# A fused Fourier filter and two expert layers: the start of the kernel loaded and ordered in another way

## The chip, the cores and the metric

The kernel runs on one core of a Trainium2 chip. The metric is device time in microseconds (us) for one launch; the smaller the better. The engines are TensorE (PE: matmuls; PEld: its weight loads, which overlap them), VectorE (DVE), ScalarE (ACT), GpSimd (POOL) and SyncE (SP), which in this kernel does nothing but issue DMAs. Each engine works through its own queue in order. PSUM is the memory that matmuls write to, here eight banks of 128 x 512 f32; SBUF is the on-chip memory of 128 partitions.

## The reference

Three steps in a row, cut here to what matters: a Fourier transform along the sequence, a product with a complex filter, the transform back; then two expert layers, the first with a piecewise quadratic in the middle, the second with `silu`.

```python
X = np.fft.rfft(x, axis=1)                     # x: 2 x 3008 x 256
Y = X * (filt_r + 1j * filt_i)[None, :, :]
x = np.fft.irfft(Y, n=3008, axis=1).reshape(6016, 256)
h = x @ w_in                                   # 256 -> 2048
g = np.where(h >= 1, h, np.where(h <= -1, 0.0, (h + 1) ** 2 / 4))
x = g @ w_out                                  # 2048 -> 256
h = x @ w_in2
out = (h * (1 / (1 + np.exp(-h)))) @ w_out2
```

## The kernel before

The transform of length 3008 = 47 x 64 is done with small transform matrices. The work is cut into 32 **items** (`items`: 16 groups of 16 channels for each of two sequences). The first `HEAD` = 17 items form the **head** of the program and are the subject here; the other 15 are woven into the first expert layer later on. An item i of the head goes through these steps, each put at a time slot `t` of the table `agenda`:

- `load_x(i)` and `load_f(i)`: DMAs on SP. `x` is 96 partitions x 512 f32, the filter 64 partitions x 768 f32, 196.6 KB each. The filter is needed in both halves of the partitions. In the head only its first half is loaded, and `twin_f` (ACT) copies it to partitions 64 to 127. The 16 items of the first sequence load `x` straight into the large tile `Z1`; the filter has a ring of six buffers.
- `fwd_n1` (PE, matrix `fwd1`), `turn_fwd` (DVE, a transpose `t<-h`), `fwd_n2` (PE, matrix `fwd2`, a part of the constant tile `dft_sb`).
- `signs` (POOL) multiplies the filter's second part by the constant `sgn`, and `filter_` (DVE) multiplies by both filter parts, `y<-h,f`.
- `swap_add`: two copies on ACT (`s<-y`) swap the partition halves of the second product, and POOL adds them to the first (`y<-y,s`). For the last four items of the head (`LAST` = 4) it is left out, and `inv_n2` instead does two matmuls, one with the matrix `inv2_swap`, whose rows are swapped, and one with `inv2`.
- `inv_n2` (PE, `o_b<-y`), `turn_inv` (DVE, a transpose `Z<-o_b`).

When the head is done, four calls of `prep_x` (PE, `h<-dft_sb,Z`, with `inv1`) make the input of the first expert layer for two blocks of 502 tokens. Then the layer's **slots** follow, from `t = NB` = 24 on: in each, `up` makes 128 of the 2048 inner rows of a block (six matmuls, `h<-x,wh`), ACT and DVE form the quadratic, `split_g` splits the result into a rounded part `gh` and a rest `gl`, and `down` (six matmuls, `o_a<-gh`) adds to the output. `down` runs `LAG` = 5 slots behind `up`. The weights are converted from 64-bit words by `read_weight` (ACT, two operations), `form_weight` (DVE, three operations on `we` and `wa`, then POOL) and split by `split_weight` (ACT `wh`, then POOL `wl`).

The order on each engine is that of the code up to slot `HOLD`; from there the class `Planner` keeps the code's order on PE, and chooses the order on the other engines by its own estimate of when each operation can start and is due. `head_banks` in the diff adds two PSUM banks to the four that the ring `h` has. A DMA waits, beside its buffer, for a semaphore that an earlier DMA used: there are eight of them, so at most eight DMAs are under way.

Of the kernel before, what the change touches and what calls it, by code (L numbers as in the profile page):

```python
# [9 lines left out]
F32 = mybir.dt.float32  # L10
# [5 lines left out]
AF = mybir.ActivationFunctionType  # L16
# [10 lines left out]
K1 = N1 // 2 + 1  # L27
# [5 lines left out]
UTOK = 2 * N1  # L33
# [20 lines left out]
def _constants():  # L54
# [31 lines left out]
    dft[:, 256:384] = inv2.reshape(128, 128)  # L86
    dft[:, 384:384 + UTOK] = inv1.reshape(128, UTOK)
    dft[:, 384 + UTOK:384 + UTOK + K1] = sgn
    dft[:, 384 + UTOK + K1:] = np.roll(inv2.reshape(128, 128), 64, 0)
    return dft.astype(np.float32)  # L90


# [194 lines left out]
def tile_fft_conv_moe_moe(  # L287
# [11 lines left out]
    nc = Planner(tc.nc)  # L299
    ctx.enter_context(tc.manual_schedule())  # L300
    HEAD, LAG, EARLY = 17, 5, 12
    LAST = 4
# [19 lines left out]

    for tag in ("gh", "gl"):
        rings[tag] = [mp.tile([128, PMAX], F32R, tag=tag, name=f"{tag}_{i}", bufs=LAG - 1) for i in range(LAG - 1)]
    rings["ob"] = [mp.tile([128, PMAX], F32, tag="ob", name=f"ob_{i}", bufs=3) for i in range(3)]

    def make_ring(tag, n, pool, shape, dtype):
# [31 lines left out]

    nc.scalar.dma_start(fwd1, dft[:96, :128])  # L360
    fwd2 = dft_sb[:, 0:128]
    inv2 = dft_sb[:, 128:256]
    inv1 = dft_sb[:, 256:256 + UTOK]
    sgn = dft_sb[:, 256 + UTOK:]


    weights, cv = {}, {}
# [67 lines left out]
    def load_f(i):  # L435
        c, b = items[i]
        ft[i] = rot("f")
        for h in range(1 if i < HEAD else 2):
            nc.sync.dma_start(ft[i][h * 64:(h + 1) * 64], filt[c])

    def twin_f(i):

        if i < HEAD:
            nc.scalar.activation(ft[i][64:128], ft[i][0:64], AF.Copy)

    mats = {}

# [63 lines left out]
        st[i] = y.rearrange("p (d k) -> p d k", k=K1), v  # L513

    def swap_add(i):
        if HEAD - LAST <= i < HEAD:
            return
        y, v = st[i]
        yf = y.rearrange("p d k -> p (d k)")
        s = rot("s")  # L520
        nc.scalar.activation(s[0:64], v[64:128], AF.Copy)
        nc.scalar.activation(s[64:128], v[0:64], AF.Copy)
        nc.gpsimd.tensor_tensor(yf, yf, s, ALU.add)
        st[i] = y

    def inv_n2(i):
        z = zps[i % len(zps)][:, :, :K1]
        if HEAD - LAST <= i < HEAD:
# [587 lines left out]
    def at(t, fn, *args):  # L1116
        agenda.setdefault(t, []).append((fn, args))
# [5 lines left out]
    def plan_weight(t, m, f, pool):  # L1123
        at(t, fetch_weight, m, f)
        at(t + CR, read_weight, m, f)
        at(t + CF, form_weight, m, f)
        at(t + CS, lambda: split_weight(m, f, pool()))


    DONE = HEAD + 4  # L1130
    for i in range(HEAD):
        if i >= 3:
            at(i - 3, load_x, i)
        if i >= 2:
            at(i - 2, load_f, i)
    for t in range(DONE + 1):
        for fn, d in ((twin_f, 0), (fwd_n2, 2), (inv_n2, 4), (fwd_n1, 0), (turn_fwd, 1), (signs, 1), (turn_inv, 5), (filter_, 2), (swap_add, 2)):
            if 0 <= t - d < HEAD:
                at(t, fn, t - d)
    at(8, lambda: nc.sync.dma_start(inv2_swap, dft[:, 384 + UTOK + K1:]))  # L1140
    at(NB - P0, prep_x, 0, 0)
    at(NB - P1, prep_x, 1, 0)
    at(NB - P2, prep_x, 0, 1)
# [87 lines left out]
    open_dp("dpa", 2, 6, 3, 2)  # L1231
    warm = dp.tile([128, 512], BF16, name="warm", bufs=1)
    nc.vector.memset(warm, 0.0)
    ps = rot("h")
    for _ in range(WARM):
        nc.tensor.matmul(ps, warm[:, :128], warm, start=True, stop=True)
    clear_pads("a")
    load_x(0)
    load_x(1)
    nc.scalar.dma_start(dft_sb, dft[:, 128:384 + UTOK + K1])  # L1240

    nc.scalar.activation(warm[:, :1], warm[:, :1], AF.Silu)
    load_f(0)
    load_x(2)
    load_f(1)
    inv2_swap = dp.tile([128, 128], F32, name="inv2_swap", bufs=1)
# [7 lines left out]
    def stages(t):  # L1254
        nonlocal late
        if t == max(NB, DONE + 1):
            dctx.close()
# [10 lines left out]
        if t == END:  # L1268
# [121 lines left out]
```

## Time and profile before

| what | value |
|---|---|
| median of 3 runs | 1087.36 us (1086.96 to 1087.63) |
| the profiled execution: its own time | 1088.39 us |
| the profiled execution: span from first to last instruction | 1086.6 us |
| busy, as a share of the span | PE 99%, PEld 81%, DVE 85%, ACT 84%, POOL 21% |
| head and `prep_x` (first product to the first `up`) | 3.75 to 53.50 us |

The span is 1.8 us shorter than the execution's own time. The page's times start at the span's start. A row of the timeline gives the start, the length, the engine, the operation with output and inputs, and, in brackets, how long the engine sat idle before it and what ended that. An f32 matmul of the head shows as two records (x2). The ends of PE's records are modelled and overlap the next one, so the time a matmul takes is read from the distance of two starts.

### The profile page before, as it was taken

The numbers are of one execution on the slowest core, as the hardware profiler recorded it, in microseconds if no ns is written. First come the engines' busy times: TensorE is split into PE (matmuls) and PEld (weight loads), VectorE is DVE, ScalarE is ACT, GpSimd is POOL, SyncE is SP. The second block draws the span as 40 slices with busy tenths as digits, with TensorE's granted clock in tenths as the row PEclk, the third lists the DMA queues.
The fourth block names the chain that finished last, engine by engine and source line by source line (L and its number), as shares of the span: only waits on it lengthen the run. The fifth ranks groups of instructions, "written<-read, shape, count | busy, mean of one in ns | idle before, by whom it ended". The sixth has DMA issues, their size and how long they took to land.

```text
span 1086.6 us, 14688 instructions
## 1 busy us (share of the span) xinstructions
PE 1077.3 (99%) x4797; PEld 880.5 (81%) x4797; DVE 920.3 (85%) x1528; ACT 909.6 (84%) x1700; POOL 224.9 (21%) x208
## 2 busy tenths in 40 slices
PE   9999999999999999999999999999999999999997
PEld 4678888888888888887878878888888888888885
DVE  7989667877779786768887688999999999999988
ACT  6699778878778878879999889889889898889885
POOL 5656234666522110004433000000000000000000
PEclk9999999999999999999999999999999999999999
DMA  9634032435221000115686753433434333332401
GB/s 203 153 97 146 21 124 75 147 116 147 89 87 59 20 1 1 39 39 175 222 275 218 296 168 104 148 110 109 145 113 140 131 106 118 134 103 102 140 1 38
DMA packets 57884, 126.50 MB, mean 116 GB/s; under 512 B 6192, under 2 KB 30224, under 8 KB 57808
## 3 DMA queue, kind: packets, MB, share of 16 engines
q1 hardware_dynamic: 57552, 125.33, 35.9%
q8 instruction: 37, 0.61, 0.2%
q14 instruction: 39, 0.32, 0.1%
q10 hardware_dynamic: 256, 0.24, 0.1%
HBM read 94.35 MB, written 31.20 MB: 116 GB/s over the span
## 4 chain that ended last, share of the span: by engine, by line
PE 88%; DVE 5%; ACT 3%; DMA 1%; issue 1%; SPq 0%; POOL 0%; DVEq 0%; ACTq 0%
PE h L172 44%; PE o_a L172 24%; PE o_b L172 20%; DVE gl L172 1%; ACT gh L172 1%; DVE xr L172 1%; DVE y L172 1%; DMA f<-in_filt_dram 1%; ACT c L172 0%; ACT rawb L172 0%; DVE t L172 0%; SPq L172 0%; DMA inv_swap<-in_dft_dram 0%; DMA raw<-in_moe_w_in_dram 0%; DVE h L172 0%
## 5 line engine op out<-in xcount | busy, mean ns | idle before, releaser
L172 PE MATMUL h<-xr,ur 128*128 128x502 f32 (+1 forms) x816 | 227.6, 389 | 0.2
L172 PEld LDWEIGHTS h<-xr,ur 128*128 128x128 f32 x816 | 153.4, 189 | 33.3 <-ACT sl_g L172 0.8
L172 PE MATMUL o_a<-gh,wh 128*128 128x502 f32 (+1 forms) x395 | 154.4, 391 | 0.9 <-DVE sl_wh L172 0.7
L172 PE MATMUL o_a<-gl,wh 128*128 128x502 f32 (+1 forms) x395 | 154.2, 390 | 0.5 <-DVE gl L172 0.5
L172 PE MATMUL o_a<-gh,wl 128*128 128x502 f32 (+1 forms) x395 | 154.1, 390 | 0.0
L172 PE MATMUL o_b<-gh,wh 128*128 128x502 f32 (+1 forms) x292 | 114.2, 391 | 0.0
L172 PE MATMUL o_b<-gh,wl 128*128 128x502 f32 (+1 forms) x292 | 113.8, 390 | 0.0
L172 PE MATMUL o_b<-gl,wh 128*128 128x502 f32 (+1 forms) x292 | 113.7, 389 | 0.0
L172 ACT ACTIVATE gh<-sl_g 128x502 fp32r<-128x502 f32 (+1 forms) x141 | 87.4, 620 | 18.0 <-PE o_a L172 8.1
L172 DVE TENSOR_TENSOR gl<-sl_g,gh 128x502 fp32r<-128x502 f32 (+1 forms) x141 | 94.8, 673 | 8.9 <-ACT gh L172 8.7
L172 DVE TENSOR_TENSOR gl<-h,gh 128x502 fp32r<-128x502 f32 (+1 forms) x122 | 82.1, 673 | 12.7 <-ACT gh L172 11.6
L172 ACT ACTIVATE u<-h 128x502 f32<-128x502 f32 (+1 forms) x122 | 71.3, 585 | 23.4 <-PE h L172 22.6
L172 DVE SCALAR_TENSOR_TENSOR h<-u,h 128x502 f32<-128x502 f32 (+1 forms) x84 | 57.1, 681 | 39.5 <-ACT u L172 38.7
L172 PEld LDWEIGHTS o_a<-gh,wh 128*128 128x128 f32 x395 | 74.4, 188 | 17.1 <-ACT gh L172 1.5
L172 PEld LDWEIGHTS o_a<-gl,wh 128*128 128x128 f32 x395 | 74.4, 188 | 16.6 <-DVE gl L172 1.5
L172 PEld LDWEIGHTS o_a<-gh,wl 128*128 128x128 f32 x395 | 74.3, 188 | 15.2
L172 ACT ACTIVATE gh<-h 128x502 fp32r<-128x502 f32 (+1 forms) x122 | 71.3, 585 | 4.9 <-DVE h L172 1.6
L172 ACT ACTIVATE u<-u 128x502 f32<-128x502 f32 (+1 forms) x115 | 71.6, 623 | 2.9 <-DVE u L172 0.6
L172 POOL TENSOR_TENSOR w2s<-w2s 128x448 fp32r<-128x448 f32 x32 | 41.3, 1306 | 139.8 <-DVE w2s L172 114.7
L172 PE MATMUL h<-xb,wh 128*128 128x502 f32 (+1 forms) x212 | 65.7, 391 | 0.8 <-ACT g L172 0.8
L172 PEld LDWEIGHTS o_b<-gh,wh 128*128 128x128 f32 x292 | 55.0, 188 | 11.4 <-ACT o_b L172 0.4
L172 PEld LDWEIGHTS o_b<-gh,wl 128*128 128x128 f32 x292 | 54.9, 188 | 11.5
(368 smaller groups left out, 2599.3 us busy)
## 6 DMA issues: line engine op xcount, KB each, us to landing
ur<-w2u SPq DMA_DIRECT2D x48, 896.0 KB, 4.7
f<-in_filt_dram SPq DMA_DIRECT2D x47, 192.0 KB, 4.8
w2u<-w2s SPq DMA_DIRECT2D x16, 448.0 KB, 3.2
raw<-in_moe_w_in_dram SPq DMA_DIRECT2D x16, 256.0 KB, 2.8
raw<-in_moe_w_out_dram SPq DMA_DIRECT2D x16, 256.0 KB, 3.2
w2d<-wa SPq DMA_DIRECT2D x16, 256.0 KB, 3.4
w2s<-w2d SPq DMA_DIRECT2D x32, 128.0 KB, 3.0
w2v<-w2s SPq DMA_DIRECT2D x16, 256.0 KB, 2.6
```

The source lines that it names most:

```text
L172: op = Op(engine, lambda: call(*args, **kwargs), busy, until, port)
```

## The change

- The head's filter is loaded twice, into partitions 0 to 63 and 64 to 127; `twin_f` is gone.
- The constants are loaded in pieces: `fwd2` and `sgn` first (on ACT's queue), `inv2` and `inv2_swap` behind the second filter (on SP's), `inv1` at slot 6. For that their columns change places.
- `x` is loaded five items ahead and the filter three (before: three and two); three `x` are issued ahead of the first filter.
- The ring `h` has six banks during the head.
- The first two items (`FIRST` = 2) do their swap by products, as the last four do; `filter_` of item 0 comes one slot later.
- `form_weight` and `split_weight` come two slots later for the first weight, one later for the second. `HOLD` is 19 instead of 22.
- `down` is 3 slots behind `up` for the first slots; at slots 24 and 28 no `down` is done, so that it is 4 and then 5 behind, as before.

```diff
-        for h in range(1 if i < HEAD else 2):
+        for h in range(2):
             nc.sync.dma_start(ft[i][h * 64:(h + 1) * 64], filt[c])
...
-        if HEAD - LAST <= i < HEAD:
+        if i < FIRST or HEAD - LAST <= i < HEAD:
             return
...
-        at(t + CF, form_weight, m, f)
-        at(t + CS, lambda: split_weight(m, f, pool()))
+        late = [2, 1][f] if f < 2 else 0
+        at(t + CF + late, form_weight, m, f)
+        at(t + CS + late, lambda: split_weight(m, f, pool()))
...
+    AHEAD_F, AHEAD_X = 3, 5
     for t in range(DONE + 1):
-        for fn, d in ((twin_f, 0), (fwd_n2, 2), (inv_n2, 4), (fwd_n1, 0), (turn_fwd, 1), (signs, 1), (turn_inv, 5), (filter_, 2), (swap_add, 2)):
-            if 0 <= t - d < HEAD:
-                at(t, fn, t - d)
-    at(8, lambda: nc.sync.dma_start(inv2_swap, dft[:, 384 + UTOK + K1:]))
+        for fn, d in ((fwd_n2, 2), (inv_n2, 4), (fwd_n1, 0), (turn_fwd, 1), (signs, 1), (turn_inv, 5), (filter_, 2), (swap_add, 2)):
+            for i in range(HEAD):
+                if t == i + d + (fn in (filter_, swap_add) and i < 1):
+                    at(t, fn, i)
+    for i in range(AHEAD_F, HEAD):
+        if i >= AHEAD_X:
+            at(i - AHEAD_X, load_x, i)
+        at(i - AHEAD_F, load_f, i)
+    at(6, lambda: nc.sync.dma_start(inv1, dft[:, 512 + K1:]))
...
+    def lag(i):
+        return min(LAG, 3 + max(0, i - 20) // 4)
+
     late, gp, lctx = None, None, ExitStack()
-    marks, PLAN, HOLD = {}, 3, NB - 2
+    marks, PLAN, HOLD = {}, 3, 19
...
-            if i >= LAG:
-                down(*slots[i - LAG])
+            if i >= lag(i) and (i == 0 or lag(i) <= lag(i - 1)):
+                down(*slots[i - lag(i)])
```

What this does to the order is seen best at three places. In the names, a trailing number is that of a buffer; `Z_117` is where `x` lands, `f_163` to `f_168` are the six filter buffers.

First, SP's queue at the start of the program, before:

```order
L172 DMA Z_117<-in_x_dram 96x512 x2
L172 DMA f_163<-in_filt_dram 64x768
L172 DMA Z_117<-in_x_dram 96x512
L172 DMA f_164<-in_filt_dram 64x768
L172 DMA f_165<-in_filt_dram 64x768
L172 DMA Z_117<-in_x_dram 96x512
```

and now:

```order
L172 DMA Z_117<-in_x_dram 96x512 x3
L172 DMA f_163<-in_filt_dram 64x768 x2
L172 DMA Z_117<-in_x_dram 96x512
L172 DMA f_164<-in_filt_dram 64x768 x2
L172 DMA dft_sb<-in_dft_dram 128x128
L172 DMA inv_swap<-in_dft_dram 128x128
L172 DMA Z_117<-in_x_dram 96x512
L172 DMA f_165<-in_filt_dram 64x768 x2
```

Each filter is two DMAs now, `x` stands ahead of it, and the two matrices of the swap by products come behind the second filter. In the steady head SP has three DMAs for an item instead of two.

Second, PE from the third `fwd_n1` to the first two `inv_n2` (`o_b`), before:

```order
L172 MATMUL h_91<-Z_117,fwd_114 128x512
L172 MATMUL h_92<-t_1_170,dft_sb 128x384
L172 MATMUL h_93<-Z_117,fwd_114 128x512
L172 MATMUL h_94<-t_0_169,dft_sb 128x384
L172 MATMUL o_b_112<-y_171,dft_sb 128x16x24
L172 MATMUL h_91<-Z_117,fwd_114 128x512
L172 MATMUL h_92<-t_1_170,dft_sb 128x384
L172 MATMUL o_b_113<-y_172,dft_sb 128x16x24
```

and now:

```order
L172 MATMUL o_a_110<-Z_117,fwd_114 128x512
L172 MATMUL o_a_111<-t_1_170,dft_sb 128x384
L172 MATMUL h_91<-Z_117,fwd_114 128x512
L172 MATMUL h_92<-t_0_169,dft_sb 128x384
L172 MATMUL o_b_112<-y_171,inv_swap 128x16x24
L172 MATMUL o_b_112<-y_171,dft_sb 128x16x24
L172 MATMUL h_93<-Z_117,fwd_114 128x512
L172 MATMUL h_94<-t_1_170,dft_sb 128x384
L172 MATMUL o_b_113<-y_172,inv_swap 128x16x24
L172 MATMUL o_b_113<-y_172,dft_sb 128x16x24
```

The sequence is the same but for one matmul more in each of the first two `inv_n2`.

Third, DVE at the end of the head, around the transpose `t` of item 16, before:

```order
L172 TENSOR_TENSOR y_173<-h_94,f_165 128x384 x2
L172 TENSOR_SCALAR we_106<-raw_107 128x512
L172 TENSOR_SCALAR wa_103<-wa_103 128x512
L172 SCALAR_TENSOR_TENSOR wa_103<-wa_103,we_106 128x512
L172 STREAM_TRANSPOSE t_0_169<-h_91 128x512
L172 STREAM_TRANSPOSE Z_116<-o_b_112 128x16x16x2
```

and now:

```order
L172 TENSOR_TENSOR y_173<-h_92,f_165 128x384 x2
L172 STREAM_TRANSPOSE t_0_169<-h_93 128x512
L172 STREAM_TRANSPOSE Z_116<-o_b_112 128x16x16x2
L172 TENSOR_TENSOR y_171<-h_94,f_166 128x384 x2
L172 STREAM_TRANSPOSE Z_116<-o_b_113 128x16x16x2
L172 TENSOR_TENSOR y_172<-o_a_110,f_167 128x384 x2
L172 TENSOR_SCALAR we_106<-raw_107 128x512
```

The three operations on the first weight stood ahead of the last transpose of the head and stand behind the last `filter_` now. The third weight's last DVE operation (`wa_105<-wa_105,we_106`) moves too: before, it stood ahead of both splits of the second `prep_x` pair; now it stands behind the first `h_94<-u_97,h_94` of the slots.

## Rows read from the trace of the kernel before

**Rows 1.** The page's first part: busy time, share of the span, instructions.

```profile
PE 1077.3 (99%) x4797; PEld 880.5 (81%) x4797; DVE 920.3 (85%) x1528; ACT 909.6 (84%) x1700; POOL 224.9 (21%) x208
```

**Rows 2.** Waits of PE over the span: us in total, times, longest.

```profile
PE h L172 <- DVE gl L172: 0.6, 1, 0.6
...
PE o_b L172 <- POOL y L172: 0.4, 1, 0.4
```

**Rows 3.** Timeline of PE, start: start, length, operation, [idle before <- what ended it].

```profile
3.75 4.07 PE L172 MATMUL h<-Z,fwd 96*128 96x512 f32 x4
7.61 1.49 PE L172 MATMUL h<-t,dft_sb 128*128 128x384 f32 x2
...
10.37 0.81 PE L172 MATMUL h<-t,dft_sb 128*128 128x384 f32 x2
...
11.96 0.81 PE L172 MATMUL h<-t,dft_sb 128*128 128x384 f32 x2
13.12 0.91 PE L172 MATMUL o_b<-y,dft_sb 128*128 128x384 f32 x2 [0.35 <-POOL y L172]
13.87 1.02 PE L172 MATMUL h<-Z,fwd 96*128 96x512 f32 x2
```

**Rows 4.** The same timeline of ACT, POOL and DVE.

```profile
7.08 0.84 ACT L172 ACTIVATE f<-f 64x768 f32<-64x768 f32 x1 [2.91 <-DMA f<-in_filt_dram]
...
10.94 1.05 ACT L172 ACTIVATE s<-y 64x384 f32<-64x384 f32 x2
...
8.00 0.86 POOL L172 TENSOR_TENSOR f<-f,dft_sb 128x384 f32<-128x384 f32 x1 [7.56 <-ACT f L172]
...
12.07 1.00 POOL L172 TENSOR_TENSOR y<-y,s 128x384 f32<-128x384 f32 x1 [1.43 <-ACT s L172]
...
10.57 0.72 DVE L172 STREAM_TRANSPOSE t<-h 128x512 f32<-128x512 f32 x1 [0.41 <-PE h L172]
11.27 0.96 DVE L172 TENSOR_TENSOR y<-h,f 128x768 f32<-128x768 f32 x1
```

**Rows 5.** Timeline of PE in the steady head, one item of it.

```profile
28.94 1.02 PE L172 MATMUL h<-Z,fwd 96*128 96x512 f32 x2
...
30.45 0.81 PE L172 MATMUL o_b<-y,dft_sb 128*128 128x384 f32 x2
31.09 1.02 PE L172 MATMUL h<-Z,fwd 96*128 96x512 f32 x2
```

**Rows 6.** Stretch: length, PE, PEld, DVE, ACT, POOL busy, PEclk, DMA share, GB/s.

```profile
7.60:10.30 2.70, 2.70 (x5) 1.35 (x4) 1.67 (x2) 1.39 (x3) 1.40 (x2) 1.00 1.06 205
...
22.00:30.00 8.00, 8.00 (x23) 4.21 (x23) 8.00 (x12) 6.57 (x11) 6.70 (x9) 1.00 1.06 214
```

**Rows 7.** DMA: GB/s in slices of 0.375 us (225 to 240), filter loads (0 to 40).

```profile
GB/s 0 0 44 0 0 0 0 0 0 0 0 0 74 295 260 262 322 303 57 0 0 0 0 0 0 0 0 0 0 0 0 0 0 104 221 369 265 216 191 221
...
f<-in_filt_dram SPq DMA_DIRECT2D x17, 192.0 KB, 6.1
```

**Rows 8.** Timelines of PE and DVE at the head's end.

```profile
41.86 0.81 PE L172 MATMUL o_b<-y,dft_sb 128*128 128x384 f32 x2
42.91 0.91 PE L172 MATMUL h<-t,dft_sb 128*128 128x384 f32 x2 [0.24 <-DVE t L172]
...
42.15 0.71 DVE L172 STREAM_TRANSPOSE t<-h 128x512 f32<-128x512 f32 x1
```

**Rows 9.** Waits between 40 and 62 us, PE's weight loads: total, times, longest.

```profile
PEld o_b L172 <- DVE Z L172: 1.0, 3, 0.5
```

**Rows 10.** Timelines of PE, DVE and POOL at the first slots.

```profile
53.50 0.70 PE L172 MATMUL h<-x,wh 128*128 128x502 f32 x2
...
59.85 0.73 PE L172 MATMUL h<-x,wh 128*128 128x502 f32 x2 [0.60 <-DVE gl L172]
...
56.98 0.69 DVE L172 SCALAR_TENSOR_TENSOR h<-u,h 128x502 f32<-128x502 f32 x1
...
54.92 1.30 POOL L172 TENSOR_TENSOR wl<-wa,wh 128x512 fp32r<-128x512 f32 x1 [0.46 <-ACT wh L172]
```

More of the change, by code (lines that the diff above doesn't have):

```diff
@@ L85, in _constants @@
     dft[:, 128:256] = fwd2.reshape(128, 128)
[L86 to L89, printed above, removed]
+    dft[:, 256:256 + K1] = sgn
+    dft[:, 256 + K1:384 + K1] = inv2.reshape(128, 128)
+    dft[:, 384 + K1:512 + K1] = np.roll(inv2.reshape(128, 128), 64, 0)
+    dft[:, 512 + K1:] = inv1.reshape(128, UTOK)
     return dft.astype(np.float32)
@@ L301, in tile_fft_conv_moe_moe @@
     HEAD, LAG, EARLY = 17, 5, 12
-    LAST = 4
+    FIRST, LAST = 2, 4
     SP, P0, P1, P2, P3, NBX, SZ = 27, 5, 3, 2, 2, 8, 7
@@ L324, in tile_fft_conv_moe_moe @@
         rings[tag] = [mp.tile([128, PMAX], F32R, tag=tag, name=f"{tag}_{i}", bufs=LAG - 1) for i in range(LAG - 1)]
+    head_banks = lambda: rings["h"].extend(out_bank[t] for t in ("a0", "a1"))
     rings["ob"] = [mp.tile([128, PMAX], F32, tag="ob", name=f"ob_{i}", bufs=3) for i in range(3)]
@@ L361, in tile_fft_conv_moe_moe @@
     fwd2 = dft_sb[:, 0:128]
-    inv2 = dft_sb[:, 128:256]
-    inv1 = dft_sb[:, 256:256 + UTOK]
-    sgn = dft_sb[:, 256 + UTOK:]
+    sgn = dft_sb[:, 128:128 + K1]
+    inv2 = dft_sb[:, 128 + K1:256 + K1]
+    inv1 = dft_sb[:, 256 + K1:]
     weights, cv = {}, {}
@@ L437, in load_f @@
         ft[i] = rot("f")
-        for h in range(1 if i < HEAD else 2):
+        for h in range(2):
             nc.sync.dma_start(ft[i][h * 64:(h + 1) * 64], filt[c])
-    def twin_f(i):
-        if i < HEAD:
-            nc.scalar.activation(ft[i][64:128], ft[i][0:64], AF.Copy)
     mats = {}
@@ L527, in inv_n2 @@
         z = zps[i % len(zps)][:, :, :K1]
-        if HEAD - LAST <= i < HEAD:
+        if i < FIRST or HEAD - LAST <= i < HEAD:
             y, v = st.pop(i)
@@ L1125, in plan_weight @@
         at(t + CR, read_weight, m, f)
-        at(t + CF, form_weight, m, f)
-        at(t + CS, lambda: split_weight(m, f, pool()))
+        late = [2, 1][f] if f < 2 else 0
+        at(t + CF + late, form_weight, m, f)
+        at(t + CS + late, lambda: split_weight(m, f, pool()))
     DONE = HEAD + 4
[L1131 to L1135, printed above, removed]
-    for t in range(DONE + 1):
-        for fn, d in ((twin_f, 0), (fwd_n2, 2), (inv_n2, 4), (fwd_n1, 0), (turn_fwd, 1), (signs, 1), (turn_inv, 5), (filter_, 2), (swap_add, 2)):
-            if 0 <= t - d < HEAD:
-                at(t, fn, t - d)
-    at(8, lambda: nc.sync.dma_start(inv2_swap, dft[:, 384 + UTOK + K1:]))
+    AHEAD_F, AHEAD_X = 3, 5
+    for t in range(DONE + 1):
+        for fn, d in ((fwd_n2, 2), (inv_n2, 4), (fwd_n1, 0), (turn_fwd, 1), (signs, 1), (turn_inv, 5), (filter_, 2), (swap_add, 2)):
[7 more added lines that the diff above has]
+    at(6, lambda: nc.sync.dma_start(inv1, dft[:, 512 + K1:]))
     at(NB - P0, prep_x, 0, 0)
@@ L1233, in tile_fft_conv_moe_moe @@
     nc.vector.memset(warm, 0.0)
+    head_banks()
     ps = rot("h")
@@ L1237, in tile_fft_conv_moe_moe @@
     clear_pads("a")
+    inv2_swap = dp.tile([128, 128], F32, name="inv2_swap", bufs=1)
     load_x(0)
     load_x(1)
-    nc.scalar.dma_start(dft_sb, dft[:, 128:384 + UTOK + K1])
+    load_x(2)
+    nc.scalar.dma_start(dft_sb[:, :128 + K1], dft[:, 128:256 + K1])
     nc.scalar.activation(warm[:, :1], warm[:, :1], AF.Silu)
     load_f(0)
-    load_x(2)
-    load_f(1)
-    inv2_swap = dp.tile([128, 128], F32, name="inv2_swap", bufs=1)
+    for i in range(1, AHEAD_F):
+        if i + 2 < AHEAD_X:
+            load_x(i + 2)
+        load_f(i)
+        if i == 1:
+            nc.sync.dma_start(inv2, dft[:, 256 + K1:384 + K1])
+            nc.sync.dma_start(inv2_swap, dft[:, 384 + K1:512 + K1])
     def h_ring(*more):
@@ L1256, in stages @@
         if t == max(NB, DONE + 1):
+            h_ring()
             dctx.close()
```

## The prediction

> **What bounds the kernel now.** I read the page's busy times first: PE is busy 99% of the span [rows 1], so only PE's own work and its few waits count. The list of PE's waits holds two that this change can touch, 0.6 us for `gl` and 0.4 us for POOL's sum [rows 2]; the timeline then gives their places. Up to 13.12 us PE is in the **start**: its first product begins at 3.75, and there `fwd_n2` of item 0 begins at 7.61 with a length of 1.49, while the same operation at 10.37 has 0.81 [rows 3]. The column of the granted clock prints 1.00 there [rows 6]; by the lengths the products up to about 10.37 run at the lower of TensorE's two levels (1.2 GHz) and those behind it at the upper (2.4 GHz). At 13.12 the first `inv_n2` waits for POOL. From 13.87 on the **steady head** runs: one item takes from 28.94 to 31.09, 2.15 us, which is `fwd_n1` and two products of 0.64 each (30.45 to 31.09), without a gap [rows 5]. DVE is busy 8.00 of 8.00 us there as well (22 to 30), and the DMA share is 1.06 at 214 GB/s [rows 6]: three resources are near their end at once. At the **head's end** PE waits for a transpose on DVE [rows 8] and its weight loads wait for other transposes [rows 9]; in the **first slots** it waits once, at 59.85 [rows 10].
>
> Behind slot 30 the order on PE, DVE, ACT and POOL is the same in both kernels but for buffer numbers, so what the start gains or loses is carried to the end unchanged, and nothing is to be won behind it.
>
> **The change part by part.** The sum is made against the profiled execution (span 1086.6, own time 1088.39, so 1.8 us outside the span, and 1.0 us above the median of 1087.36); the difference is then put on the median.
>
> *Two swaps by products.* Each adds one product to PE, of the same shape as the one from 30.45 to 31.09 [rows 5], 0.64 us: +1.28 us. PE is the bound there, so all of it is on the path.
>
> *The wait for POOL's sum goes.* `fwd_n2` of item 2 starts at 11.96 and takes 0.64, so PE is free at 12.60 and starts `inv_n2` at 13.12: 0.52 us, and its start-up (13.12 to 13.87 is 0.75 instead of 0.64 [rows 3]) costs 0.11 more. What stands behind the wait: the filter lands, ACT copies it (0.84, from 7.08), POOL does the signs (0.86, from 8.00), DVE the filter, ACT two copies (1.05, from 10.94, behind another filter copy), POOL the sum (1.00, to 13.07 [rows 4]). With products the chain ends at DVE's filter. DVE's new order there puts the transpose of item 2 first (10.57 to 11.2), then the filter of item 0 (0.96), so `y` is there at 12.2, ahead of 12.60. Next late would be `inv2_swap`: 1.8 MB stand in the queue up to it, less than 9 us at 214 GB/s, so by about 11 us. -0.6 us.
>
> *ACT's 17 filter copies go* (0.84 each), and POOL loses two sums. ACT is 6.57 of 8.00 busy in the steady head [rows 6] and not the bound: nothing by itself.
>
> *A second DMA for each filter.* An item takes 3 x 196.6 = 590 KB instead of 393. In 2.15 us that is 274 GB/s. The row of the steady head has 214 with the DMA share at 1.06 [rows 6], and a filter load takes 6.1 us to land there [rows 7], so the queue is full now. The nearest rows for the new mix are items behind the head, which load both halves and one `x`: the slices of one such item read 295, 260, 262, 322, 303, on average 288, those of the next 221 to 191 around a peak of 369, on average 247 [rows 7]. At 288 an item takes 2.05 us, at 247 2.39, at 214 2.76. What hides an excess is the lead of the loads: up to the second half of filter 2 some 2.2 MB land behind 3.75 us, at 260 GB/s by 12.2; it is needed 3.8 us (0.86 + 0.92 + 1.05 + 1.00, the chain above) ahead of its `inv_n2` at about 18.0, so by 14.2. The lead of 2 us covers 13 items up to 2.15 + 2.0 / 13 = 2.30 us each, 256 GB/s. I take the middle of 247 and 288, 267 GB/s (2.21 us), as nearest to the new mix: 0 us. Ends: 0 at 288, 13 x (2.76 - 2.30) = +6.0 at 214. A gain isn't in it, since PE and DVE hold the pace.
>
> A rule of the Trainium skill bears on this: "SBUF — State Buffer", section "Door 1: The DMA port swizzle (why `[64,N]` ≈ `[32,N]`)", says that partitions 0 to 63 reach only eight of the sixteen DMA ports, and 64 to 127 the other eight. By that rule the second half would cross ports that the first leaves free, an item would take no longer than the 393 KB at 214 GB/s do now (1.84 us), and this term would be 0; without it the queue's rate of 214 would hold and the term be +6.0. No run here shows the head with both halves yet.
>
> *x ahead, six banks, constants in pieces.* The third `fwd_n1` and what follows find their `x` earlier, but up to 10.37 PE has work without a gap worth naming, at the lower clock. Nothing in the change shortens that work. If the clock rose earlier, the kernel before couldn't use it, since `inv_n2` waits for POOL until 13.12 whatever PE does; the changed one could. The work from 7.61 to 10.37 (2.76 us) would take half, so the ends are 0 and -1.4. That the clock rises at another time in other executions is likely, as nothing ties it to an instruction; I take -0.3, near the end without a gain.
>
> *The first weight formed later.* DVE's three operations no longer stand ahead of the transpose of item 16, which started at 42.15 [rows 8]. PE is free at 42.50 (41.86 + 0.64) and goes on at 42.91: -0.41. The weight loads' waits for `Z` transposes are 1.0 us in three pieces, the longest 0.5 [rows 9]; one of them is a PE gap, behind the first `prep_x`. Together -0.4 to -0.9; I take -0.7. The weight itself is needed at 53.50 and is some 4 us early either way.
>
> *Downs three slots behind.* It adds and removes no work. The wait of 0.60 at 59.85 [rows 10] goes, since a `down` stands between the fourth and fifth `up`. But the third weight is late now: its last DVE operation stands behind `h<-u,h`, which came 3.48 us after the first `up` (56.98 - 53.50), and would come 2.9 to 3.5 behind it. From there 0.69 + 0.69 on DVE, 1.30 on POOL, some 0.6 on ACT, 1.30 on POOL [rows 10]: 7.5 to 8.1 us behind the first `up`. PE asks for it at 4 x 1.37 + 1.37 + 0.46 = 7.3 (an `up` or `down` of six matmuls takes 1.37). So a wait of 0.2 to 0.8 takes the place of 0.60. Queued behind it on PE are all later ups and downs. Ends -0.6 and +0.4; I take 0. The two slots without a `down` shorten PE's slot to 1.37 us, less than ACT needs for one; a wait of up to 0.5 could come there, and I take 0.
>
> Sum: +1.28 - 0.6 + 0 - 0.3 - 0.7 + 0 = -0.3 us. On the median of 1087.36: 1087.0.
>
> **The rivals.** *The queue becomes the bound (slower).* If both halves load at less than 256 GB/s, every item of the steady head is late by the excess, and PE waits for POOL's sum or DVE's filter, behind DMA. For: share 1.06 now, and the head's rate of 214. Against: the slices at 260 to 322 with the same mix. Midway between 214 and 247, at 230, an item takes 2.56 us: 13 x 0.26 = +3.4, 1090.4; at 214 1093.
>
> *The start uses an earlier clock, and the first slots lose their wait (faster).* -0.3 becomes -1.4, the 0.60 goes: 1087.0 - 1.1 - 0.6 = 1085.3. For: the chain that held 13.12 is gone. Against: nothing in the diff changes the work at the lower clock, and the third weight is late.
>
> *The third weight holds the slots (little).* With a wait of 0.8 and another at the two slots without `down`, +0.9: 1087.9. For: DVE's new order. Against: the wait at 59.85 leaves.
>
> *The change doesn't take PE's path at all:* the copies that it removes were never on it behind 13.87, so the sum is only +1.28 against three small waits. That is the forecast itself.
>
> **How the numbers follow.** Forecast, within 1 us of 1087.0: 0.58. Queue: 0.20. Clock and slots: 0.15. Third weight: 0.07. 0.2% is 2.2 us, about what a measurement of this kernel can tell from no change. Below 1085.2 lies a little under half of the third case and a part of the unknown in the first: 0.12. Above 1089.5 lies most of the queue's case: 0.17. The range goes from 1085.3 (clock and slots) to 1090.4 (the queue at 230 GB/s), and leaves out about one in ten on each side.
>
> **What would show it.** In the profile after: the first `inv_n2` starts near 12.6 and waits for no POOL; the second `fwd_n1` behind it is some 0.7 us later than now by itself; steady items keep 2.15 us, at about 270 GB/s, and no wait for `f` shows on DVE or POOL. The gap at 42.5 is gone; near the fifth `up` PE waits for `wl` or `wh`, not for `gl`. It is wrong if items take over 2.2 us, if the clock's rise moves to before 9 us, or if PE waits in the slots for more than 1 us.

## The result and the profile after

The changed kernel is slower: 1093.80 us (median of 6 executions, 1091.45 to 1098.64) against 1087.53 (6 executions of the kernel before beside it, 1086.96 to 1087.89). The ratio is 1.0061, 95% interval 1.0052 to 1.0071. The forecast was 1087.0 and the range ended at 1090.4, so it was wrong, on the slow side.

The profiled execution of the changed kernel took 1092.25 us, with a span of 1090.5 us: 3.9 us more than that of the kernel before (1088.39, 1086.6). The first `up` starts at 57.28 us instead of 53.50 [rows 10], 3.78 us later. From there to the last product of the program it is 1028.7 us, and 1028.2 before. So the time is lost ahead of the first `up`. The medians are 6.3 us apart, since this execution is one of the shorter ones of the changed kernel and that of the kernel before lies above its median; a second profile of each is read below. Of the six executions of the changed kernel the two longest (1095.75 and 1098.64 us) have the lowest mean granted clock (0.998 and 0.995, the others 1.000).

The start is close to the forecast. PE's timeline there (start, length, engine, operation, records), against [rows 3]:

```profile
7.60 1.49 PE L172 MATMUL h<-t,dft_sb 128*128 128x384 f32 x2
...
9.93 0.81 PE L172 MATMUL o_a<-t,dft_sb 128*128 128x384 f32 x2
...
12.08 0.81 PE L172 MATMUL o_b<-y,inv_swap 128*128 128x384 f32 x2
12.73 0.81 PE L172 MATMUL o_b<-y,dft_sb 128*128 128x384 f32 x2
...
16.17 1.02 PE L172 MATMUL o_a<-Z,fwd 96*128 96x512 f32 x2
18.32 1.02 PE L172 MATMUL h<-Z,fwd 96*128 96x512 f32 x2
```

The first `inv_n2` starts at 12.08, two products long, and waits for nothing; the kernel before had 13.12 and a wait for POOL. The first product of the sixth item stands at 16.17 (16.02 before), the next 2.15 us behind it: up to here the change costs 0.15 us. Then the items grow longer:

```profile
24.78 1.09 PE L172 MATMUL h<-Z,fwd 96*128 96x512 f32 x2
...
32.11 1.12 PE L172 MATMUL h<-Z,fwd 96*128 96x512 f32 x2 [0.19 <-DMA Z<-in_x_dram]
...
37.54 1.13 PE L172 MATMUL o_a<-Z,fwd 96*128 96x512 f32 x2 [0.64 <-DMA Z<-in_x_dram]
...
42.50 1.13 PE L172 MATMUL h<-xin,fwd 96*128 96x512 f32 x2
...
51.73 0.91 PE L172 MATMUL o_b<-y,inv_swap 128*128 128x384 f32 x2 [1.62 <-DVE Z L172]
```

From 24.78 to 42.50 are seven items, 2.53 us each instead of 2.15 [rows 5]. PE waits there for `x` itself, not for POOL or DVE, and its weight loads wait for `x` too. The last item's first product stands 2.8 us later than in the kernel before (39.71). At 51.73 PE waits another 1.6 us, now for a transpose on DVE. POOL and DVE before it:

```profile
47.60 1.00 POOL L172 TENSOR_TENSOR f<-f,dft_sb 128x384 f32<-128x384 f32 x1 [2.56 <-DMA f<-in_filt_dram]
...
48.63 1.02 DVE L172 TENSOR_TENSOR y<-o_a,f 128x384 f32<-128x384 f32 x2 [1.91 <-POOL f L172]
49.57 0.42 DVE L172 TENSOR_SCALAR we<-raw 128x512 int32<-128x512 int32 x1
...
50.36 0.69 DVE L172 SCALAR_TENSOR_TENSOR wa<-wa,we 128x512 int32<-128x512 int32 x1
50.97 1.31 DVE L172 STREAM_TRANSPOSE Z<-o_b 128x512 f32<-128x512 f32 x2
```

The transpose stands on DVE behind the filter of the last item, whose load is late, and behind the three operations on the first weight (49.57 to 50.97), which the change itself put in that place. By these starts some 1.4 of the 1.6 us are theirs; that is an estimate, and the run that puts them back (e11 below) makes DVE wait for the weight instead. The waits of all engines up to 55 us (total, times, longest) show the loads too:

```profile
POOL f L172 <- DMA f<-in_filt_dram: 19.1, 14, 7.0
ACT wa L172 <- DMA raw<-in_moe_w_out_dram: 7.8, 2, 6.0
...
PEld h L172 <- DMA Z<-in_x_dram: 3.6, 6, 0.8
```

And the table by stretch (length, PE, PEld, DVE, ACT, POOL busy, PEclk, DMA share, GB/s), against [rows 6]:

```profile
14.00:22.00 8.00, 8.00 (x24) 4.19 (x23) 7.70 (x11) 3.56 (x7) 6.39 (x7) 1.00 1.05 244
22.00:30.00 8.00, 8.00 (x22) 3.72 (x21) 7.76 (x12) 3.75 (x8) 6.81 (x8) 1.00 1.05 246
30.00:38.00 8.00, 7.17 (x19) 3.17 (x18) 6.88 (x10) 3.13 (x6) 5.98 (x7) 1.00 1.05 246
```

The DMA engines are as full as before (1.05) and move 246 GB/s where they moved 214. An item's 590 KB take 2.40 us at that rate. (From 24.78 to 42.50 it is 242 GB/s, and 4.29 MB land, 0.16 MB more than seven items have; a constant of 47 KB is among them.) ACT is 3.75 of 8.00 busy instead of 6.57: the copies are gone, from an engine for which PE did not wait in the steady head.

### The profile page after: what moved, and what is told of

Its sections match the earlier page's. It is cut to its first block, busy times and chain, and to the rows that moved or that the text cites. A ratio compares the mean times of both kernels' runs of the same rounds, so it can differ in the third digit from the quotient of the medians.

```text
span 1090.5 us, 14708 instructions
## 1 busy us (share of the span) xinstructions
PE 1079.3 (99%) x4801; PEld 880.8 (81%) x4801; DVE 919.8 (84%) x1528; ACT 894.2 (82%) x1679; POOL 227.7 (21%) x206
## 4 chain that ended last, share of the span: by engine, by line
PE 85%; DVE 5%; ACT 4%; DMA 4%; issue 1%; SPq 0%; POOL 0%; DVEq 0%; ACTq 0%; POOLq 0%
PE h L172 42%; PE o_a L172 23%; PE o_b L172 19%; DMA f<-in_filt_dram 2%; DMA Z<-in_x_dram 2%; DVE gl L172 1%; ACT gh L172 1%; ACT c L172 1%; DVE xr L172 1%; ACT w2s L172 1%; ACT rawb L172 1%; DVE sl_g L172 0%; SPq L172 0%; DVE h L172 0%; ACT u L172 0%
```

## The experiments

Theory A: the second filter half makes the DMA transfers the bound of the head. Rival B: the new order at the head's end and in the first slots costs the time. Theory A has two forms that had to be told apart later: the price is one of bytes, or one of how they are loaded. All kernels compute the whole. The rate is that of the stretch 22 to 30 us; "last item" is the start of the last `fwd_n1` of the head, "rest" the time from the first `up` to the last product. Ratios are against the kernel before, run beside each.

| run | ratio, 95% interval | GB/s | last item | first `up` | rest |
|---|---|---|---|---|---|
| before | | 214 | 39.71 | 53.50 | 1028.2 |
| after | 1.0061 [1.0052, 1.0071] | 246 | 42.50 | 57.28 | 1028.7 |
| e1 one half | 1.0007 [0.9998, 1.0017] | 199 | 40.15 | 53.02 | 1028.3 |
| e2 two halves alone | 1.0059 [1.0043, 1.0076] | 250 | 45.53 | 60.19 | 1028.2 |
| e3 four items doubled | 1.0024 [1.0014, 1.0033] | 217 | 41.42 | 54.30 | 1028.3 |
| e4 late forms, downs | 1.0012 [1.0003, 1.0021] | 203 | 39.66 | 52.64 | 1030.6 |
| e5 spare half, high | 1.0061 [1.0041, 1.0081] | 250 | 45.72 | 58.69 | 1028.4 |
| e6 spare half, low | 1.0110 [1.0090, 1.0130] | 218 | 50.44 | 65.11 | 1028.2 |
| e7 half by ACT | 1.0087 [1.0067, 1.0107] | 226 | 46.61 | 60.71 | 1030.2 |
| e8 one load, read twice | 1.0989 [1.0970, 1.1007] | 71 | | 160.82 | 1030.9 |
| e9 start alone | 1.0020 [1.0011, 1.0029] | 230 | 39.46 | 53.26 | 1030.3 |
| e10 without products | 1.0068 [1.0055, 1.0081] | 201 | 43.38 | 57.18 | 1028.4 |
| e11 forms not late | 1.0065 [1.0049, 1.0081] | 235 | 44.25 | 62.65 | 1027.7 |
| e12 start, filters in place | 1.0028 [1.0017, 1.0040] | 208 | 40.22 | 54.01 | 1030.5 |
| e13 one half, in place | 1.0016 [1.0007, 1.0025] | 206 | 40.38 | 53.25 | 1028.4 |
| e14 one wide load | 1.0002 [0.9993, 1.0011] | 261 | 40.47 | 53.34 | 1028.8 |

**The halves, and all the rest.** The changed kernel with one half and ACT's copy (e1), the kernel before with the second half and no copy (e2), the changed kernel with both halves for its first four items (e3), and the kernel before with the late forms, `HOLD` 19 and the earlier downs (e4).

```diff
 # e1, and e3 with DOUBLE = 4, from after; twin_f is planned again
+    DOUBLE = 0
...
-        for h in range(2):
+        for h in range(1 if DOUBLE <= i < HEAD else 2):
 # e2, from before; twin_f does nothing
-        for h in range(1 if i < HEAD else 2):
+        for h in range(2):
```

> The changed kernel, but the head's filter is loaded into the lower half only and copied up by ACT, as before; all else stays (order of x, constants in pieces, two swaps by products, downs three slots behind, later weights). Theory A (the DMA queue is the bound of the head, because of the second half): items go back to 2.15 us each, no wait for x on PE, first up near 53.5 us, time 1086.3 to 1088. Rival B (the new order at the head's end and in the first slots costs the time): the gap of 1.6 us in front of the last inverse product and the 0.6 us wait for wl stay, time above 1090.

> The kernel before, with the filter loaded into both halves in the head and no ACT copy; nothing else. Theory A: the queue stays full at about 245 GB/s up to some 47 us, items of 2.3 to 2.5 us, time 1091 to 1096. Rival B: 1087 to 1088, since the order of before stays.

> The changed kernel with both halves loaded for the first four items only and ACT's copy for the other thirteen. Theory A: the start of the changed kernel (first inverse product at 12.1 us) with steady items of 2.15 us, time 1085.5 to 1087.5. Rival B: above 1090, like the changed kernel.

> The kernel before with the later forming of the first two weights, the planner from slot 19, and the first downs three slots behind; the loads are those of before. Theory A: 1086.5 to 1088, no more than 0.7 us from before. Rival B: above 1090.

Taking the second half out of the change gives the time back (1088.00 us, items of 2.15 us, first `up` at 53.02). Putting it alone into the kernel before costs as much as the whole change (1094.25). Theory A holds, and B falls as the cause of the loss: e4 is 1.5 us slower by its median, more than the 0.7 that I had allowed, but none of that lies ahead of the first `up`. PE's waits in e2 (total, times, longest):

```profile
PE h L172 <- DMA Z<-in_x_dram: 3.6, 4, 2.3
PE h L172 <- DMA xin<-in_x_dram: 2.2, 1, 2.2
```

In e2, PE waits for `x`, which stands behind the doubled filters. The first `up` comes at 60.19 there and at 57.28 in the changed kernel, where `x` is five items ahead. But the two medians are only 0.45 us apart, and in the second profile of the changed kernel the first `up` stands at 57.96; so whether the change softens what its own second half costs is not shown. e3 was expected to be no slower than before and lost 2 us; its profile shows one wait of 0.98 us for POOL's sum at 19.14 and no loss of rate. Its cause was not followed further.

**Bytes, partitions or queue.** The kernel before with one more load of 196.6 KB per item into a scratch buffer that nobody reads, in partitions 64 to 127 (e5) or 0 to 63 (e6); the changed kernel with the second half issued on ACT's queue (e7).

```diff
 # e5, from before; e6 with [0:64]
+        if i < HEAD:
+            nc.sync.dma_start(rot("extra")[64:128], filt[c])
...
 # e7, from after
+            q = nc.scalar if h and i < HEAD else nc.sync
-            nc.sync.dma_start(ft[i][h * 64:(h + 1) * 64], filt[c])
+            q.dma_start(ft[i][h * 64:(h + 1) * 64], filt[c])
```

> The kernel before, order and ScalarE copies untouched; only a further load of 196.6 KB per item of the head goes to a scratch buffer in partitions 64 to 127, which nobody reads. If bytes on the DMA engines are what costs, this gives the 245 GB/s and 2.4 us per item that the two halves gave, and 1091 to 1095 us. If it is something that the second half does to its readers (a wait for the second of two transfers), the extra bytes alone cost nothing: 2.15 us per item and 1087.0 to 1088.5 us.

> As the run with the spare load in partitions 64 to 127, but the spare load goes to partitions 0 to 63, where x and the filter land too. If the rate hangs on which partitions are written (in the kernel before, whose loads of the head all lie in partitions 0 to 95, the stretch 22 to 30 went at 214 GB/s with the queue full, against 246 with both halves in use), this one stays at 205 to 220 GB/s: 2.7 to 2.9 us per item and 1096 to 1101 us. If the rate is one of bytes alone, it equals the other run: 240 to 250 GB/s, 2.4 us per item, 1091 to 1095 us.

> The changed kernel, with the second half of each of the head's 17 filters issued by ScalarE in place of SyncE, so that the two halves stand in two queues. If SyncE's queue (its order, or how much one queue keeps under way) is the bound, the two queues together go faster: 2.15 to 2.2 us per item, the last first product of the head at 39.7 to 40.5, 1087 to 1089 us. If it is the 16 DMA engines, nothing is gained: 240 to 250 GB/s in the stretch 22 to 30, last first product at 42 to 43, 1091 to 1096 us.

The stretch 22 to 30 of e5, of e6 and of e7, in the columns of the table by stretch:

```profile
22.00:30.00 8.00, 8.00 (x22) 3.27 (x21) 7.14 (x11) 6.49 (x10) 6.37 (x8) 1.00 1.06 250
```

```profile
22.00:30.00 8.00, 7.12 (x19) 3.09 (x18) 6.43 (x9) 5.54 (x10) 5.35 (x7) 1.00 1.05 218
```

```profile
22.00:30.00 8.00, 6.91 (x20) 3.63 (x20) 6.72 (x10) 3.13 (x6) 6.05 (x7) 1.00 1.05 226
```

In all three the DMA engines are full. e5, whose extra bytes serve nothing and delay no reader but through the queue, costs what the change costs. The same bytes into the low partitions go at 218 GB/s instead of 250: the two runs differ in nothing but where the transfer lands, and that sets the rate, by 15% here, and 5.3 us of the time (1094.43 and 1099.77, two executions each). A second queue doesn't help: 226 GB/s and 1097.27 us, slower than both outcomes that I had named. Some 2 us of that lie behind the first `up`; why the rate is lower than the 246 of one queue was not followed. So it is neither SP's queue nor the number of bytes alone.

**One load in place of two.** e8 fills all 128 partitions by one load whose source has a leading dimension of two with stride zero. e14 keeps the filter twice in DRAM, in 128 rows laid out before the launch, and loads these in one transfer; it, too, moves the bytes of the change.

```diff
 # e8, from after; in the head only
...
+            twice = bass.AP(f.tensor, f.offset, [[0, 2], [2 * XS, 64], [1, 2 * XS]])
+            nc.sync.dma_start(ft[i].rearrange("p s x -> p (s x)"), twice)
 # e14, from after; in the head only
...
+            nc.sync.dma_start(ft[i], filt[c])
...
-        "filt": np.ascontiguousarray(fl).reshape(NCH, N2, 2, XS),
+        "filt": np.concatenate([fl, fl], 1).reshape(NCH, 2 * N2, 2, XS),
```

> The changed kernel, with the two loads of a filter in the head replaced by one load that writes all 128 partitions (its source is read twice). The same bytes. If the price of the second half is one of bytes, the stretch 22 to 30 stays at 240 to 250 GB/s and the time at 1091 to 1095 us. If it is one of two narrow loads that share part of the way into the partitions, one wide load goes at 270 GB/s or more: 2.15 us per item, last first product of the head at 39.7 to 40.5, 1086.5 to 1088.5 us.

> The changed kernel, with the filter kept twice in DRAM (128 rows in place of 64, arranged before the launch), so that one load with 128 rows of its own fills both halves of the partitions. The same bytes and all of the changed kernel's order. In the earlier run with one load the source was read twice through a leading dimension of two, and the load went at some 50 GB/s with 0.13 of the DMA engines busy. If two narrow loads one after the other are what holds the rate at 245 GB/s, one load over all partitions goes at 274 GB/s or more in the stretch 22 to 30: 2.15 us per item, last first product of the head at 39.5 to 40.5, 1086.5 to 1089 us. If the rate is bound by the bytes or by x, whose loads stay in partitions 0 to 95, it stays at 240 to 260 GB/s and the time at 1091 to 1095 us.

e8 between 14 and 22 us, then e14 from 14 to 30, in the same columns:

```profile
14.00:22.00 8.00, 3.35 (x4) 1.18 (x4) 0.96 (x1) 0.00 (x0) 0.99 (x1) 0.50 0.13 51
```

```profile
14.00:22.00 8.00, 8.00 (x24) 4.21 (x23) 6.91 (x10) 3.13 (x6) 5.33 (x6) 1.00 1.05 261
22.00:30.00 8.00, 8.00 (x24) 4.32 (x23) 8.00 (x13) 4.18 (x8) 7.22 (x9) 1.00 1.05 261
```

e8 tested something else than it was meant to: the share of 0.13 is that of two of the sixteen DMA engines, and the load crawls at 51 GB/s. The Trainium skill has this in "DMA: Bandwidth & Descriptors", section "Rules for kernel authors": a leading zero-stride dimension of c copies keeps a transfer on at most c engines. Here c is 2 and the row agrees, with 0.13 x 16 = 2.1.

e14 is the deciding run. Its rate lies between the two outcomes that I had named (274 or more, 240 to 260), its time in the first. At 261 GB/s an item's loads take 2.26 us, their lead covers that, all items keep 2.15 us and PE has no wait for a load. The time is that of the kernel before (1088.04 us; 1087.91 beside it). So the loss was not the price of the bytes but of the way they were loaded. e14 differs from the change in three things: one transfer instead of two, 128 source rows read once instead of 64 read twice, and, since at most eight DMAs are under way, more bytes under way. Which of them gives the 261 instead of 246 was not separated. The second copy in DRAM is made before the launch and isn't in the time.

**The parts of the start.** The start of the change alone with one half, forms and downs as before (e9); the same without products (`FIRST` = 0, e10); the same as e9 with the loads in the order of the kernel before (e12); e1 with that order (e13); the changed kernel with `late` = 0 (e11).

```diff
 # e10, from e9
-    FIRST, LAST = 2, 4
+    FIRST, LAST = 0, 4
 # e12 from e9, e13 from e1; the first loads in the old order too
-    AHEAD_F, AHEAD_X = 3, 5
+    AHEAD_F, AHEAD_X = 2, 3
 # e11, from after
-        late = [2, 1][f] if f < 2 else 0
+        late = 0
```

> The changed kernel's start alone (products for the first two swaps, constants in pieces, x ahead), with one filter half and ScalarE's copy as in the kernel before, and with the forms of the weights and the downs as before. By the theory that the second half holds all of the loss, this is the kernel before with some 0.5 us less at its start: first up of the moe at 52.6 to 53.2 (53.50 before), 1086.0 to 1087.8 us. By the rival that the new order itself costs time, it loses what the one-half run lost: 1088 us or more.

> The start alone as in the run beside it, but with the first two swaps added by GpSimd again, as before. By the prediction's sum the two products cost 1.28 us of TensorE and take away a wait of 0.6 us for GpSimd: without them the sixth item's first product starts 1.28 us earlier, or 0.7 us earlier if the wait is back; against the start alone the whole is 0.6 to 0.7 us shorter. If the products lie in time in which TensorE waits for loads anyway, the two start the same item within 0.3 us and the times are equal within 0.4 us.

> The changed kernel with both halves, its two first weights formed where they were before (not two and one slots later). In the changed kernel TensorE waits 1.62 us at 51.7 for the last item, and VectorE works on the weights for 0.8 us right before that item's part. If the late forms are a cause, that wait falls to 0.8 us or less and the first up comes 0.8 us earlier (at 56.5 in place of 57.3), 1092 to 1093.5 us. If the late filter alone is the cause, the wait stays at 1.3 to 1.9 us, the first up at 57 to 57.6; or VectorE now waits for the weights' own late loads and everything is later still, 1094 to 1096 us.

> As the start alone (one filter half, products for the first two swaps, constants in pieces, forms and downs as before), but with the loads in the order of the kernel before: two x, the first filter, the third x, the second filter, and then two and three items ahead in place of three and five. If the x that the change puts ahead of the filters is what the start alone lost (GpSimd's sum waited 1.1 us at 15.8 there, and without products 4.9 us at 9.8), no wait of over 0.5 us is left on TensorE before 53 us and the time is 1086.3 to 1087.8 us. If products and constants lose by themselves, it stays at 1089 to 1091 us.

> All of the change but the second half and the x ahead: products, constants in pieces, late forms, downs three slots behind the ups, with the loads in the order of the kernel before. If the x ahead is a loss of its own, this is the best of the kernels: 1085.8 to 1087.3 us, with the wait of 0.6 us for the third weight left. If the downs and late forms lose by themselves (they gave 1088.95 us alone), it stays at 1088 to 1089.5 us.

PE and ACT in e10, then PE and DVE in e11:

```profile
9.49 0.81 PE L172 MATMUL h<-t,dft_sb 128*128 128x384 f32 x2
15.15 1.65 PE L172 MATMUL o_b<-y,dft_sb 128*128 128x384 f32 x2 [4.86 <-POOL y L172]
...
11.00 0.84 ACT L172 ACTIVATE f<-f 64x768 f32<-64x768 f32 x1 [1.41 <-DMA f<-in_filt_dram]
12.12 0.84 ACT L172 ACTIVATE f<-f 64x768 f32<-64x768 f32 x1 [0.28 <-DMA f<-in_filt_dram]
12.97 2.14 ACT L172 ACTIVATE s<-y 64x384 f32<-64x384 f32 x4
```

```profile
50.78 0.91 PE L172 MATMUL o_a<-t,dft_sb 128*128 128x384 f32 x2 [3.47 <-DVE t L172]
...
48.25 0.43 DVE L172 TENSOR_SCALAR we<-raw 128x512 int32<-128x512 int32 x1 [2.55 <-DMA raw<-in_moe_w_out_dram]
```

In e10 PE waits 4.86 us for POOL's sum of the first item, and behind that wait it runs at its lower clock (the `inv_n2` at 15.15 takes 1.65 instead of 0.81). DVE has the first item's product ready at 9.85; but ACT makes its two copies for the swap only from 12.97, behind its copies of the filters of items 2 and 3, whose loads keep it waiting. My expectation of a gain of 0.6 to 0.7 us from taking the products out had the wrong sign: beside ACT's filter copies and the new order of loads, leaving them out costs 4.4 us (1094.34 against 1089.91). The changed kernel has no filter copies on ACT, so e10 doesn't say what the products are worth there. In e11 DVE waits 2.55 us for the weight at 48.25, the transpose behind it comes late, and that makes PE wait 3.47 us. This profile is the longest of its four executions (1096.82; two took 1092.19 and 1092.72), and the medians of e11 and of the change (1094.57, 1093.80) can't be told apart: that the late forms help is not shown, only that they are not the loss.

The times of e9, e12 and e13 (1089.91, 1090.67, 1089.27 us) are those of the second outcome of each expectation, in which the new order loses time by itself. But their first `up` (53.26, 54.01, 53.25) is at most 0.5 us behind that of the kernel before in its first profile, while e9 and e12 are 2.4 and 2.9 us slower. The column "rest" has it: 1030.3 and 1030.5 instead of 1028.2, as in e4. Four second profiles were taken for that.

**Second profiles**, of the unchanged files of before, e9, e13 and after.

> A second profile of the kernel before, unchanged. In the first one the weight's load issued at 265.8 us landed after 3.6 us and nothing waited. If the landing times go with the kernel, it lands within 4 us again and TensorE has no wait of over 0.5 us between 270 and 280; if they are chance, it lands late (5 to 6.2 us, a wait of 0.9 to 1.5 us there) in some profiles of this kernel too.

> A second profile of the start alone. In its first one that load landed after 6.0 us and TensorE waited 0.95 us at 277, and GpSimd's sum came 1.08 us late at 15.8. If the landing times go with the kernel, both waits are there again, at the same places and sizes; if they are chance, one or both are gone and the time falls to 1088 to 1089 us.

> A second profile of all of the change but the second half and the x ahead, whose eleven times fell into two groups (1088.0 to 1088.3 and 1089.3 to 1090.9); the first profile was of the first group, without a wait at 277. If this one is of the second group, a late landing at 265 to 272 with a wait of 0.9 us or more at 277 would show where the 2 us lie; without one, the late loads there are not the cause of the two groups.

> A second profile of the changed kernel, whose first was among the shortest of its executions (1092.25 against a median of 1093.8). The head at 240 to 250 GB/s with the last first product at 42 to 44 and the first up at 57 to 60 would say that the spread too is made in the head; a head as in the first profile and a longer time would put it behind.

ACT in the first profile of e13 and in the second:

```profile
269.55 0.66 ACT L172 ACTIVATE wa<-early 128x512 f32<-128x512 f32 x1
```

```profile
270.86 0.67 ACT L172 ACTIVATE wa<-early 128x512 f32<-128x512 f32 x1 [2.22 <-DMA early<-in_moe_w_out_dram]
```

A weight's two loads, issued near 265 us, land after 3.7 to 3.9 us in the first profile (1088.13 us) and after 5.2 to 6.1 in the second (1089.08). In the second, ACT stands still for 2.2 us; matched product by product, PE falls 1.15 us behind the first profile at 276.7, and 0.3 in the 4 us ahead of that. The order is the same in both. In both profiles of the kernel before the loads land within 3.6 us, in both of e9 after 5.0 us or more: it goes with the kernel more than with chance, but e13 shows both, and its eleven times fall into two groups (1088.0 to 1088.3, 1089.3 to 1090.9; the second profile lies between them). What decides it stays open. e4, e9 and e12, whose "rest" is 2.1 to 2.4 us longer than that of the kernel before, have the late landing too (5.0 to 6.2 us); that it makes up all of this was not worked out. The loss of the change has none of it: its two profiles have 3.3 to 3.6 us there.

In p4 (1093.63 us) the first `up` stands at 57.96, 5.3 us behind p1's 52.64. PE in p4:

```profile
50.78 1.39 PE L172 MATMUL o_b<-y,inv_swap 128*128 128x384 f32 x2 [1.61 <-DVE Z L172]
51.96 1.48 PE L172 MATMUL o_b<-y,dft_sb 128*128 128x384 f32 x2
53.24 4.91 PE L172 MATMUL h<-dft_sb,Z 128*128 128x62 f32 x36
```

Behind the wait the products take 1.48 instead of 0.81 (in the first profile, behind the same wait, 0.81). The granted clock from 52 to 54 us reads 0.50 here, the lower of the two levels (1.2 GHz), and 1.00 in the first profile. So behind the same wait PE lost the upper level in one of two executions.

The two pairs of profiles, and e14, cut at three places of PE (us):

| stretch of PE | before | p1 | after | p4 | e14 |
|---|---|---|---|---|---|
| to the sixth item's first product | 16.02 | 15.15 | 16.17 | 16.54 | 16.79 |
| from there to the last item's first product | 23.69 | 23.69 | 26.33 | 25.02 | 23.68 |
| from there to the first `up` | 13.79 | 13.80 | 14.78 | 16.40 | 12.87 |

With the loads in time (e14) the middle stretch is as before and the last one 0.9 us shorter. Against e14 the late loads and what hangs on them cost the changed kernel 2.65 + 1.91 = 4.6 us in the first profile and 1.34 + 3.53 = 4.9 in the second.

## Why the prediction was wrong, step by step

- *A second DMA for each filter: the step that failed.* It took 267 GB/s, the middle of 247 and 288 from [rows 7], and so put the term at 0 us. The head went at 246, and the late loads cost 4.6 to 4.9 us (the table above). The two ends came from items behind the head, where the queue stands empty most of the time and a short burst is measured; the head is a full queue for 40 us. That the lower of the two came within 1 GB/s is luck: it is the mean of one such burst. The bound that the step gave itself held on both sides: above 256 GB/s no loss (e14, 261), below it a loss (246 and 250).
- *The price below that bound was too small as well.* At 246 GB/s the step's own formula gives 13 x (2.40 - 2.30) = 1.3 us. Up to the last item's first product the change loses 2.6 us in the first profile and 1.3 in the second. In the first, part of the difference is the lead, which the step put at 2 us: POOL starts on the third filter at 12.87, not at 12.2, and the `inv_n2` that needs it stands at 17.68, not at 18.0, so that by the step's own 3.8 us the lead is 1.0. The formula then gives 13 x 0.25 - 1.0 = 2.25; with the second profile's 250 GB/s and its lead of 1.7 it gives 13 x 0.21 - 1.7 = 1.0. Both are estimates. Left out altogether was the head's end: two weight loads (256 KB each, together 2.1 us at 246 GB/s) stand in the same queue, behind the last `x` but ahead of the last filter:

```profile
35.19 0.36 SPq L172 DMA_DIRECT2D xin<-in_x_dram  x1
...
38.06 0.56 SPq L172 DMA_DIRECT2D raw<-in_moe_w_in_dram  x1
38.91 0.36 SPq L172 DMA_DIRECT2D raw<-in_moe_w_out_dram  x1
40.04 1.11 SPq L172 DMA_DIRECT2D f<-in_filt_dram  x2
```

  From that filter's lateness follow POOL's signs, DVE's filter, the first weight's three operations and the transpose behind them, one wait of 1.6 us at 51.7, and in p4 the clock lost behind it: 14.78 and 16.40 us from the last item to the first `up`, where 12.87 is what loads in time give. The rival with the queue had the mechanism and the sign; at 230 GB/s it gave 1090.4, and the kernel took 1093.8 at 246.
- *The rule of the Trainium skill.* The prediction set the port rule of "SBUF — State Buffer" beside the term, and read from it that the second half would be free. The rows say it was not: an item's 590 KB took 2.40 us at 246 GB/s, where by that reading they would have taken no longer than 393 KB at 214 (1.84). The direction is in the runs (e5 against e6). The same page of the Trainium skill goes on in "Can I just issue two DMAs to hit both halves?": two transfers at once, one on each half, gave 6% over a single one, and only a single transfer over all 128 partitions reaches all ports. That speaks against the change, and the prediction did not weigh it. Here, in a queue that mixes these loads with those of `x`, the rate rose by 15% (214 to 246), and with one wide load by 22% (261); the order agrees with the Trainium skill, and the first step is larger than its 6%.
- *Products, POOL's wait, the clock.* Right in the first profiles: the wait is gone, PE rises to its upper clock at 9.9 instead of 10.4. Summed, +1.28 - 0.6 - 0.3 = +0.4 us; the sixth item's first product came 0.15 us later. In the second ones it came 1.4 later (16.54 against 15.15): there the kernel before has no such wait either, since its second and third filters land earlier and ACT's copies with them, and the clock rises no earlier in the changed kernel (10.3 in p4, 10.2 in p1). The row of `inv_n2` in p1:

```profile
12.33 0.83 PE L172 MATMUL o_b<-y,dft_sb 128*128 128x384 f32 x2
```

  So the -0.6 rests on a wait that one of two profiles has, and 13.12 is no bound that holds whatever PE does. The rival with an earlier clock shows in e9, whose sixth item started at 14.59, 1.4 us ahead of the first profile of the kernel before; a wait of 0.92 us for POOL's sum and the start-up behind it took most of that back (last item at 39.46 instead of 39.71). The clock was up by 7 us in both profiles of e9 and of e13 and only near 10 in both of the kernel before and of the changed one: in these eight it goes with the kernel, not with the execution, and why stays open.
- *The first weight later.* Right where the loads are in time: from the last item's first product to the first `up` it is 12.87 us in e1 and in e14, against 13.79 before and 13.80 in e9, which has the old forms; -0.7 was taken, -0.9 measured. In the change itself it is 14.78, since the last filter is late.
- *Downs three slots behind.* Right: PE waits 0.60 us for `wl` at 65.59 instead of 0.60 for `gl` at 59.85 [rows 10], and nothing else comes in the first slots. The row:

```profile
65.59 0.50 PE L172 MATMUL h<-x,wl 128*128 128x502 f32 x1 [0.60 <-POOL wl L172]
```

With the rate at 261, then, the rest of the sum is not contradicted: e14 measured 1.0002 [0.9993, 1.0011], where -0.3 us was forecast. Its parts came out otherwise: +0.8 and +1.6 us at the start, against the two profiles of the kernel before, where +0.4 was forecast, and -0.9 at the head's end, where -0.7 was. So a part of that agreement is luck. No run measured faster than the kernel before.

## What to carry to other kernels

Before an idle engine's copy is replaced by a second load, look at the DMA share of that very stretch: at 1.05 the queue has no room, however idle the reader, and whether further bytes cost time hangs on the rate that the new mix gets (here 246 to 250 GB/s lost, 261 did not). That rate must be read from a full queue, not from bursts. If the data is wanted in both halves of the partitions, one transfer over all of them, from a copy in DRAM with the partitions as the leading dimension, did better here than two; it gained nothing over ACT's copy. A stage that is bound by its loads also delays what stands behind it in the queue, and a wait at its end can cost the clock as well, as in p4.

## What the runs showed of the hardware

- With the DMA engines full (share 1.05 to 1.07, stretch 22 to 30 us), the DMA moved 199 to 230 GB/s with one filter half (230 and 209 in the two profiles of e9), 218 with a third load into partitions 0 to 63, 235 to 250 with both halves in use from one queue, 226 from two, and 261 with one wide load in place of two.
- A load with a leading dimension of two kept a share of 0.13 of the DMA engines busy, that of two of sixteen: 51 GB/s.
- The same pair of loads, issued at the same place of the program, landed after 3 to 4 us or after 5 to 6 us; between the two profiles of e13 the time from the first `up` on differs by 1.7 us.
- The same wait of 1.6 us was followed by products at the upper clock in one execution of the changed kernel and at the lower in another (0.81 and 1.48 us for the same operation; granted clock 1.00 and 0.50).
